# Rows of key differences for the row maxima: later loads, one load for shared keys, and a unit of eleven phases

## The chip, the cores and the metric

One NeuronCore of one Trainium2 chip runs the whole program as a single launch. The metric is the device time of one execution in microseconds. Three runs of the kernel before took 5777.38, 5781.78 and 5785.39 us; their median is 5781.78 us.

## The reference, cut to what matters

Four layers are computed one after another, A, B, A, B. Every layer normalizes its input, projects it, attends with 32 heads of 18 elements over 2048 positions, projects the result and adds it to its input. A layer of kind A has its own keys and values for each head; a layer of kind B has one key head and one value head for all 32 query heads.

```
S, D, H = 2048, 576, 32;  Dh = 18
def _A_ref(x, wqkv, wo):
    q, k, v = (x @ wqkv) split into 3 x 32 heads
    scores = einsum("bhqd,bhkd->bhqk", q, k) * Dh ** -0.5
    p = softmax(scores);  o = einsum("bhqk,bhkd->bhqd", p, v)
    return o @ wo
def _B_ref(x, wq, wk, wv, wo):      # k, v: one head
    scores = einsum("bhqd,bkd->bhqk", q, k) * Dh ** -0.5
    ...
x = x + _A_ref(layernorm(x)); x = x + _B_ref(layernorm(x))
x = x + _A_ref(layernorm(x)); x = x + _B_ref(layernorm(x))
```

All arrays are float32. Queries and keys are held as a high and a low part, so that three products of 18 rows each (54 rows) give a score in nearly full precision in one matmul.

## The kernel before, in words

**Units.** Heads are taken in pairs `p` (16 of them), and the queries in quarters `u` of 512, so that a layer has 64 units `(p, u)`. The two heads of a pair lie in partitions 0 to 63 and 64 to 127 (`a` = 0 or 1), so a matmul for one head and a matmul for the other can run side by side. A unit needs three kinds of TensorE work:

- 32 *max* matmuls (`max_mm`, L557): 128 queries against 512 keys into a PSUM tile `psm` with three buffers. VectorE reduces each to its row maxima (L580). Four of the 32 are *difference* matmuls (L570): the keys are replaced by the difference of the first two key blocks, ScalarE applies a relu (L573), and the other of the two blocks is then added and reduced in one VectorE operation (L578), so that one of two reductions is taken off VectorE. Which of the 32 they are is in `UNIT_X`.
- 32 *exp* matmuls (`exp_mm`, L787 to L797): 128 keys against 512 queries into a PSUM tile `pse` with four buffers, with the row maximum subtracted through two further rows of the query tile. ScalarE writes the exponentials (L797) to `pt`.
- 8 blocks of 512 columns of the *values* product (`pv_block`, L818): four matmuls at a time, in four column groups of the array, accumulate in `oacc`, which ScalarE copies out once a unit (L825).

**Order of the work.** The order is written out by hand in `UNIT`: a list of phases, each a string of max (`m`) and exp (`e`) matmuls with the head that they belong to, followed by a number of columns of the values product. One pass through the list is one unit: 32 `m`, 32 `e`, 4096 columns. The list before has ten phases. Max matmuls run 56 ahead of exp matmuls (`LEAD` = 14 steps of four).

**Small work by due time.** The rest is put into `todo` with a due step (`at`, L868), and `run_todo` issues at the start of a phase what is due; a step is four exp matmuls. For a unit that ends at step `b`: `max_store` at `b + NM_AT` transposes the negated maxima on VectorE (L778) and sends them to DRAM (L780); `max_rows` at `b + ROW_AT` loads them as rows of the query tile (L784); `l_part`, `l_inv`, `l_out`, `l_rows`, `o_mul`, `o_out` make and apply the reciprocal sums with GpSimd and small DMAs. The negated maxima are split into two parts on GpSimd (L158 and L773 into `hl`) before the transpose. All DMAs are issued by the one SyncE queue (SP), in program order.

**Key differences.** For each pair, `diff_in` (L599) loads parts of the keys, `diff_split` (L614) subtracts and splits them on GpSimd, `diff_out` (L624) writes them to DRAM in `kd_d`, and `diff_rows` (L631) loads them from there as 54 rows per head. The rows of pair 0 lie in the ends of two slots of `big`; those of pair `p` > 0 lie in one of two places in `xx`, by `p % 2` (`kd`, L592). In a layer of kind A the four steps of pair `p + 1` are due at steps 32p-10, 32p-7, 32p-5 and 32p-2 (L881); the max matmuls of pair `p - 1`, which read the same place, end at step 32p. In a layer of kind B they run twice, for pairs 0 and 1, though the key head is the same.

Of the kernel before, what the change touches and what calls it, by code (L numbers as in the profile page):

```python
# [17 lines left out]
DH = D // H  # L18
P = 128
NCH = S // P  # L20
NPAIR = H // 2
# [23 lines left out]

STEPS = 8
LEAD = 14
NM_AT = 3
ROW_AT = 5
SUM_AT = 3  # L50
L_AT = 5
# [10 lines left out]

UNIT = [("m0 m1 e0 e1 m1", 256), ("e1 m0 m0 e1 e0 m1", 480), ("m0 e1 m1 e0 e0 m1 e0", 448),
# [3 lines left out]
UNIT = [([(o[0], int(o[1])) for o in rows.split()], cols) for rows, cols in UNIT]  # L69

UNIT_X = (1, 9, 18, 24)


@with_exitstack
def tile_kernel(ctx: ExitStack, tc: tile.TileContext, A_x, A_wqkv, A_wo, B_x, B_wq, B_wk, B_wv, B_wo, out):
    nc = tc.nc
# [313 lines left out]
    for layer in range(4):  # L393
        is_a = layer % 2 == 0
# [79 lines left out]
        def q_slot(p):  # L474
            return (3, 5, 1)[p % 3] if is_a else (3, 4, 0)[p % 3]
# [43 lines left out]
        def ops(p):  # L519
            return big[:, q_slot(p)], big[:, k_slot(p)]  # L520
# [11 lines left out]
        for a in range(2):  # L532
            cycle = [g for rows, _ in UNIT for kind, g in rows if kind == "m"]
            n = -4 * LEAD % 32
            own = [(i, i % 32 in UNIT_X) for i in range(n, n + 32) if cycle[i % 32] == a]
            order = [None] * 16
# [8 lines left out]
        def max_place(a, i):  # L545

            p, u = divmod(i // 16, 4)
            if i < len(m_first):
                return (0, *m_first[i])
            n = i % 16  # L550
            return (p, u, *m_order[a][n]) if i >= 32 else (p, u, n // 2 % 4, n // 8 % 2 * 2 + n % 2)


        ns = STEPS * 4 * NPAIR
        m_heads = ([0, 1] * (2 * LEAD) + [g for rows, _ in UNIT for kind, g in rows if kind == "m"] * (4 * NPAIR))[:4 * ns]

        def max_mm(bank=mtile):  # L557

            i = m_done[0]
            a = m_heads[i]  # L560
            p, u, qc, kb = max_place(a, m_next[a])
            q, k = ops(p)
            if (p, u) not in mxs:
                mxs[p, u] = pool.tile([P, 32], F32, name="mx") if (p, u) < (0, 2) else mx2[u % 2]
            mx, ps = mxs[p, u], bank("psm")
            b, r = 64 * a, 16 * a + 4 * qc + kb
            c0 = u * 512 + qc * P
            if (p, u) >= (0, 2) and (a, qc, kb) in m_diff:
                k = kd(p)[b:b + 3 * DH]
                nc.tensor.matmul(ps.rearrange("p (h t) -> p h t", h=2) if p == 0 else ps, q[b:b + 3 * DH, c0:c0 + P], k,  # L570
                                 start=True, stop=True)
                t = relus[p, u, a, qc] = relu[:, :512]
                nc.scalar.activation(t, ps, AF.Relu)  # L573
            else:
                nc.tensor.matmul(ps, q[b:b + KM, c0:c0 + P], k[b:b + KM, kb * 512:(kb + 1) * 512], start=True, stop=True)  # L575
                if kb == 0 and (p, u, a, qc) in relus:
                    t = relus.pop((p, u, a, qc))
                    nc.vector.tensor_tensor_reduce(t, ps, t, 1.0, LOWEST, OP.add, OP.max, mx[:, r:r + 1])  # L578
                else:
                    nc.vector.reduce_max(mx[:, r:r + 1], ps, axis=AX.X)  # L580
            m_next[a] += 1
            m_done[0] += 1
            while m_full and i >= m_full[0][1] + 2:
                max_final(*m_full.pop()[0])
            m_count[p, u] = m_count.get((p, u), 0) + 1
            if m_count[p, u] == 32:
                assert m_next[0] == m_next[1]
                m_full.append(((p, u), i))

        relus, diffs = {}, {}  # L590

        def kd(p):  # L592
            if p == 0:
                return big[:, 1::4, 7 * 256:]
            i = p % 2 if is_a else 1
            return xx_flat[:, 512 * i:512 * i + 512]


# [30 lines left out]
                nc.sync.dma_start(kd_d[:n, i].rearrange("c (h t) -> c h t", h=2), parts_[:2 * n, c:c + 256])  # L629

        def diff_rows(p):  # L631
            for a in range(2):
                c = a * DH if is_a else 0
                src = kd_d[c:c + DH].rearrange("c i t -> (c i) t")
                if p == 0:
                    src = src.rearrange("r (h t) -> r h t", h=2)
                nc.sync.dma_start(kd(p).bitcast(F32)[64 * a:64 * a + 3 * DH], src)
# [230 lines left out]
        def at(b, f, *args):  # L868
            todo.setdefault(b, []).append((f, args))

        for p in range(NPAIR):
            for u in range(4):
                b = STEPS * (4 * p + u) + STEPS - 1
                if is_a or p or u:
                    at(b + NM_AT, max_store, p, u)
                    at(b + ROW_AT, max_rows, p, u)
                for d, f in ((SUM_AT, o_sum), (L_AT, l_part), (INV_AT, l_inv), (R_AT, l_out), (RB_AT, l_rows),
                             (MUL_AT, o_mul), (O_AT, o_out)):
                    at(b + LEAD + d, f, p, u)
            if p + 1 < NPAIR and (is_a or p == 0):  # L880
                b = max(LEAD, 32 * p - 10)  # L881
                for d, f in ((0, diff_in), (3, diff_split), (5, diff_out), (8, diff_rows)):
                    at(b + d, f, p + 1)
            if is_a and p in (0, 1):
                at(LEAD + 20 + 32 * p, load_rows, q_slot(p + 1), 2 * (p + 1) * DH, DH, 1536, S)
            if p + 1 < NPAIR:
                for i in range(4 if is_a else 2):
                    at(LEAD + 32 * (p - 1) + 1 + 8 * i if p else LEAD + 1 + 4 * i, load_part, p + 1, i)
        for c in range(5):
# [3 lines left out]
            if layer < 3:  # L893
                b = LEAD + 32 * (NPAIR - 1) + 2 * c
# [6 lines left out]
        def run_todo(st):  # L901
            for n in sorted(n for n in todo if n <= st):
                for f, args in todo.pop(n):
                    f(*args)

        b = LEAD + ns
# [10 lines left out]
        e_next = [0, 0]  # L917
# [6 lines left out]
        phase = 0  # L924
        while m_done[0] < 4 * ns:
            rows, cols = UNIT[phase % len(UNIT)]
            run_todo(LEAD + sum(e_next) // 4)
            for kind, a in rows:
                if kind == "e":
                    exp_next(a)  # L930
                elif m_done[0] < 4 * ns:
                    max_mm()
            if phase >= 2:
                pv_cols(cols)
            phase += 1
# [1 line left out]
            max_final(*m_full.pop()[0])  # L937

        while sum(e_next) < 4 * ns:
            run_todo(LEAD + sum(e_next) // 4)  # L940
            for _ in range(min(4, 4 * ns - sum(e_next))):
                exp_next(int(e_next[0] > e_next[1]))
            pv_cols(512)
# [39 lines left out]
```

## Time and profile before

| what | value |
|---|---|
| median of 3 runs | 5781.78 us (5777.38 to 5785.39) |
| the profiled execution | 5788.86 us, of which 5787.0 us are the span of its instructions |
| granted TensorE clock, mean | 0.988 |
| VectorE busy | 4942.6 us (85%) |
| ScalarE busy | 4942.4 us (85%) |
| GpSimd busy | 1839.9 us (32%) |
| DMA queue with the data | 18.2% of 16 engines' span |

How to read the lines that follow: a group of instructions is named by its line in the kernel, its engine and `out<-in`, the tiles that it writes and reads; PE is TensorE's matmuls, PEld its weight loads, DVE VectorE, ACT ScalarE, POOL GpSimd, SPq the queue that issues DMAs. A busy TensorE is not a TensorE at its peak, because a matmul counts from its start to its modelled end and neighbours overlap; the time from one start to the next tells more than a duration. A layer's attention takes most of its time: the first layer's values products run from 220.1 us, and the fourth layer's end at 5731.0 us.

### The profile page before, as it was taken

What the parts mean: (1) busy time and instruction counts of PE and PEld (TensorE: products, weight loads), DVE (VectorE), ACT (ScalarE), POOL (GpSimd) and SP (SyncE); (2) the same over time, 40 slices, a digit from 0 to 9 for tenths busy, and PEclk for the clock granted to TensorE, in tenths of its full rate; (3) what the DMA queues carried; (4) which work ended last, traced back from release to release, by engine and by line L of the source; (5) the groups of instructions that cost most, each with busy time, mean ns of one, the idle gap of its engine ahead of it and who ended that gap; (6) DMA issues with size and microseconds to landing.
All of it is one profiled execution on the core that took longest, in us unless ns stands there. A gap on an engine that the chain in (4) does not pass through costs nothing.

```text
span 5787.0 us, 140436 instructions
## 1 busy us (share of the span) xinstructions
PE 5701.3 (99%) x53790; PEld 2953.2 (51%) x53790; DVE 4942.6 (85%) x9489; ACT 4942.4 (85%) x9872; POOL 1839.9 (32%) x2406
## 2 busy tenths in 40 slices
PE   9999999999999999999999999999999999999999
PEld 8644444444744444444685444444447444444446
DVE  4788988899589999999638888998986899999995
ACT  2599999999479999999626999999993799999996
POOL 3243333333233323323312433333332332332332
PEclk9999999999999999999999999999999999999999
DMA  6321111111321010011253211111113210000002
GB/s 206 114 57 42 39 41 44 42 42 25 110 85 25 22 23 20 23 24 24 59 177 97 51 44 43 39 41 44 42 22 124 72 27 23 20 23 23 20 17 78
DMA packets 276059, 302.44 MB, mean 52 GB/s; under 512 B 135408, under 2 KB 193856, under 8 KB 266096
## 3 DMA queue, kind: packets, MB, share of 16 engines
q1 hardware_dynamic: 275384, 293.45, 18.2%
q8 instruction: 423, 6.93, 0.5%
q14 instruction: 252, 2.06, 0.1%
HBM read 169.23 MB, written 120.08 MB: 50 GB/s over the span
## 4 chain that ended last, share of the span: by engine, by line
PE 93%; DMA 2%; POOL 1%; DVE 1%; issue 1%; SPq 1%; ACT 0%; POOLq 0%; DVEq 0%; ACTq 0%
PE oacc L818 35%; PE pse L793 22%; PE psm L575 20%; PE psn L241 6%; PE psq L415 5%; PE psm L570 4%; DMA xx<-kd_d 1%; DVE mx L580 1%; PE ps L233 0%; DMA m_d<-tr 0%; DMA big<-m_d 0%; POOL big L187 0%; DMA raw<-in_B_wk_dram 0%; SPq L780 0%; POOL ev L427 0%
## 5 line engine op out<-in xcount | busy, mean ns | idle before, releaser
L797 ACT ACTIVATE pt<-pse 128x512 f32<-128x512 f32 x8192 | 4263.7, 635 | 112.8 <-PE psm L575 65.7
L580 DVE TENSOR_REDUCE mx<-psm 128x1 f32<-128x512 f32 x6208 | 3957.4, 685 | 400.5 <-PE psm L575 179.1
L575 PE MATMUL psm<-big 62*128 62x512 f32 x7200 | 2680.6, 457 | 5.5 <-DMA big<-qk_d 3.4
L793 PE MATMUL pse<-big 64*128 64x512 f32 x8192 | 2409.3, 431 | 11.9 <-DMA big<-m_d 10.0
L575 PEld LDWEIGHTS psm<-big 62*128 62x128 f32 x7200 | 1188.2, 186 | 1081.3 <-DVE mx L580 871.4
L818 PE MATMUL oacc<-pt,vbuf 128*19 128x448 f32 (+1 forms) x24560 | 1730.2, 384 | 3.5 <-DVE oc L158 3.5
L793 PEld LDWEIGHTS pse<-big 64*128 64x128 f32 x8192 | 1225.0, 187 | 362.3 <-ACT pt L797 159.8
L158 POOL TENSOR_SCALAR os<-oc 32x512 f32<-32x512 f32 x512 | 313.0, 611 | 2861.2 <-ACT oc L825 2727.1
L818 PEld LDWEIGHTS oacc<-pt,vbuf 128*19 128x19 f32 x24560 | 477.0, 98 | 672.4 <-issue 578.5
L578 DVE CUSTOM_DVE_ANT_0 relu<-psm,relu 128x512 f32<-128x512 f32 x992 | 674.6, 680 | 0.0
L573 ACT ACTIVATE relu<-psm 128x512 f32<-128x512 f32 x992 | 613.3, 618 | 62.2 <-PE psm L570 60.7
L818 PE MATMUL oacc<-pt,vy 128*19 128x352 f32 (+3 forms) x8176 | 588.0, 395 | 0.0
L570 PE MATMUL psm<-xx,big 54*128 54x512 f32 x960 | 454.6, 474 | 47.6 <-DMA xx<-kd_d 47.6
L844 POOL TENSOR_TENSOR rl<-lt,mone 128x8 f32<-128x8 f32 x256 | 422.3, 1650 | 232.8 <-DMA lt<-os 223.6
L570 PEld LDWEIGHTS psm<-xx,big 54*128 54x128 f32 x960 | 177.2, 185 | 398.6 <-DVE mx L580 372.2
L423 ACT ACTIVATE ev<-psq 128x512 fp32r<-128x512 f32 (+1 forms) x112 | 66.9, 598 | 331.7 <-PE psq L415 230.3
L857 POOL TENSOR_TENSOR os<-os,rb 96x512 f32<-96x512 f32 x256 | 329.0, 1285 | 31.3 <-DMA rb<-r_d 30.3
L835 POOL TENSOR_TENSOR os<-os,oc 96x512 f32<-96x512 f32 x256 | 327.7, 1280 | 21.3
L241 PE MATMUL psn<-wsm,xx 128*128 128x288 f32 x2240 | 308.0, 296 | 0.0
L241 PEld LDWEIGHTS psn<-wsm,xx 128*128 128x128 f32 x2240 | 298.7, 188 | 12.9 <-issue 11.3
L818 PEld LDWEIGHTS oacc<-pt,vy 128*19 128x19 f32 x8176 | 182.1, 100 | 194.2 <-issue 171.2
L429 DVE TENSOR_TENSOR ev<-psq,ev 128x512 fp32r<-128x512 f32 (+1 forms) x84 | 57.9, 690 | 213.4 <-ACT ev L423 198.6
(93 smaller groups left out, 2214.3 us busy)
## 6 DMA issues: line engine op xcount, KB each, us to landing
big<-qk_d SPq DMA_DIRECT2D x172, 432.0 KB
qk_d<-ev SPq DMA_DIRECT2D x96, 512.0 KB
qk_d<-ev SPq DMA_DIRECT2D x120, 256.0 KB
rb<-r_d SPq DMA_DIRECT2D x512, 36.0 KB
o_d<-os SPq DMA_DIRECT2D x512, 36.0 KB
m_d<-tr SPq DMA_DIRECT2D x1024, 2.0 KB
o<-o_d SPq DMA_DIRECT2D x64, 256.0 KB
xx<-qk_d SPq DMA_DIRECT2D x120, 72.0 KB
```

Source lines behind the costliest of these rows:

```text
L241: nc.tensor.matmul(ps, lhs[:, xc, :], wsm[:, wc, h * 288:(h + 1) * 288], start=i == 0, stop=i == len(TERMS) - 1)
L570: nc.tensor.matmul(ps.rearrange("p (h t) -> p h t", h=2) if p == 0 else ps, q[b:b + 3 * DH, c0:c0 + P], k, start=True, stop=True)
L573: nc.scalar.activation(t, ps, AF.Relu)
L575: nc.tensor.matmul(ps, q[b:b + KM, c0:c0 + P], k[b:b + KM, kb * 512:(kb + 1) * 512], start=True, stop=True)
L578: nc.vector.tensor_tensor_reduce(t, ps, t, 1.0, LOWEST, OP.add, OP.max, mx[:, r:r + 1])
L580: nc.vector.reduce_max(mx[:, r:r + 1], ps, axis=AX.X)
L793: nc.tensor.matmul(e, k[r:r + KE, kc * P:(kc + 1) * P], q[r:r + KE, u * 512:(u + 1) * 512], start=True, stop=True)
L797: nc.scalar.activation(pt, e, AF.Exp, scale=SCALE)
L818: nc.tensor.matmul(oacc[j:j + DH + 1, cs], v_of(kc)[:, 2 * p + a if is_a else 0, :], pts[p, u, i][:, cs], start=kc < 2 and c0 == 0, stop=k ...
L835: nc.gpsimd.tensor_tensor(t[:96], t[:96], oc[:96], op=OP.add)
L844: nc.gpsimd.tensor_tensor(rl, lts.pop((p, u)), mone, op=OP.pow)
L857: nc.gpsimd.tensor_tensor(t[:96], t[:96], rb[:96], op=OP.mult)
```

## The change

The list of phases is a new one with eleven phases, and the four difference matmuls have other places in it. `NM_AT` becomes 2.5, and the step that `run_todo` compares with is no longer rounded down, so a half step can be told. The key differences of pair `p + 1` are due two steps later, and the load of their rows four steps later (for `p` > 0). In a layer of kind B only pair 0's differences are made, and all pairs use them from the slots of `big`. `kd_pair` is bookkeeping while the program is built and leaves no instruction.

```diff
-NM_AT = 3
+NM_AT = 2.5
-UNIT = [("m0 m1 e0 e1 m1", 256), ("e1 m0 m0 e1 e0 m1", 480), ("m0 e1 m1 e0 e0 m1 e0", 448),
-        ("m0 m1 e1 e0 m0 e1", 192), ("e1 m0 m1 m0 e1", 480), ("e0 m1 e0 e0 m1 m0 e1", 416),
-        ("m0 m1 e1 m0 e1 e0 e1 m1 m0", 480), ("m1 e0 m1 e0 e1 m0", 384), ("m1 e0 e1 m0 m1 e0", 512),
-        ("e1 m0 e0 e1 m0 m1 e0", 448)]
+UNIT = [("m0 e1 e0 m1 e0 m1", 512), ("m0 e1 m1 e0 e1 m0", 416), ("e0 m1 m0 e1 e0 e1 m0", 416),
+        ("m0 m1 e1 e0 m1", 192), ("e1 m0 m1 e0 e1 m0", 544), ("m1 e0 e0 m1 m0 e1", 352), ("e0 m1 e1 m0 m0 e1", 416),
+        ("e0 m1 e0 e1 m1 m0 e1", 384), ("m0 m1", 32), ("e1 m0 e0 e1 e0 m1 m0", 448), ("e1 m0 m1 e0 e0 m1", 384)]
-UNIT_X = (1, 9, 18, 24)
+UNIT_X = (9, 17, 24, 30)
...
-                nc.tensor.matmul(ps.rearrange("p (h t) -> p h t", h=2) if p == 0 else ps, q[b:b + 3 * DH, c0:c0 + P], k,
+                nc.tensor.matmul(ps.rearrange("p (h t) -> p h t", h=2) if p == 0 or not is_a else ps,
+                                 q[b:b + 3 * DH, c0:c0 + P], k,
...
         def kd(p):
-            if p == 0:
+            if p == 0 or not is_a:
                 return big[:, 1::4, 7 * 256:]
-            i = p % 2 if is_a else 1
+            i = p % 2
...
-            if p + 1 < NPAIR and (is_a or p == 0):
-                b = max(LEAD, 32 * p - 10)
-                for d, f in ((0, diff_in), (3, diff_split), (5, diff_out), (8, diff_rows)):
-                    at(b + d, f, p + 1)
+            if p + 1 < NPAIR and is_a:
+                for d, f in ((0, diff_in), (3, diff_split), (5, diff_out), (10 if p else 8, diff_rows)):
+                    at(max(LEAD, 32 * p - 8) + d, f, p + 1)
...
-            run_todo(LEAD + sum(e_next) // 4)
+            run_todo(LEAD + sum(e_next) / 4)
```

More of the change, by code (lines that the diff above doesn't have):

```diff
@@ L568, in max_mm @@
             if (p, u) >= (0, 2) and (a, qc, kb) in m_diff:
+                assert kd_pair[p % 2 if is_a and p else 2] == (p if is_a else 0)
                 k = kd(p)[b:b + 3 * DH]
-                nc.tensor.matmul(ps.rearrange("p (h t) -> p h t", h=2) if p == 0 else ps, q[b:b + 3 * DH, c0:c0 + P], k,
+                nc.tensor.matmul(ps.rearrange("p (h t) -> p h t", h=2) if p == 0 or not is_a else ps,
+                                 q[b:b + 3 * DH, c0:c0 + P], k,
                                  start=True, stop=True)
@@ L588, in max_mm @@
                 m_full.append(((p, u), i))
-        relus, diffs = {}, {}
+        relus, diffs, kd_pair = {}, {}, {}
         def kd(p):
-            if p == 0:
+            if p == 0 or not is_a:
                 return big[:, 1::4, 7 * 256:]
-            i = p % 2 if is_a else 1
+            i = p % 2
             return xx_flat[:, 512 * i:512 * i + 512]
@@ L631, in diff_rows @@
         def diff_rows(p):
+            kd_pair[p % 2 if p else 2] = p
             for a in range(2):
@@ L939, in tile_kernel @@
         while sum(e_next) < 4 * ns:
-            run_todo(LEAD + sum(e_next) // 4)
+            run_todo(LEAD + sum(e_next) / 4)
             for _ in range(min(4, 4 * ns - sum(e_next))):
```

## The prediction

> **What bounds the kernel now.** I read the busy shares first, then who waits for whom on TensorE, then windows of the two kinds of layer, then the timeline of one unit.
>
> ```profile
> PE 5701.3 (99%) x53790; PEld 2953.2 (51%) x53790; DVE 4942.6 (85%) x9489; ACT 4942.4 (85%) x9872; POOL 1839.9 (32%) x2406
> PE psm L570 <- DMA xx<-kd_d: 47.6, 26, 2.9
> PE pse L793 <- DMA big<-m_d: 10.0, 7, 3.0
> ```
>
> TensorE is never idle for long, so every microsecond has to be found either in its few waits or in the way its matmuls follow one another. Its largest wait is for the rows of key differences: 26 times, 47.6 us. The difference matmul is written after the load that overwrites its place, so it reads, and waits for, the rows of a later pair. Whether it costs more than those 47.6 us is told by the exp matmuls (32 to a unit) that a long window holds. The first and third windows lie in layers of kind A, the others in kind B:
>
> ```profile
> 340.00:1290.00 950.00, 458.58 (x1529) 234.93 (x1529) 0.97 0.16 42
> 1660.00:2820.00 1160.00, 573.40 (x1974) 292.44 (x1972) 1.00 0.10 24
> 3220.00:4240.00 1020.00, 492.76 (x1647) 251.93 (x1645) 0.98 0.16 41
> 4545.00:5700.00 1155.00, 570.75 (x1966) 291.42 (x1963) 1.00 0.09 22
> PE psm L570 <- DMA xx<-kd_d: 21.1, 12, 2.9
> PE psm L570 <- DMA xx<-kd_d: 21.2, 12, 2.4
> ```
>
> The last two rows are the waits within the first and third window, 12 in each. Columns of the others: window, length, PE busy and count, weight loads, granted clock, DMA. A unit takes 950 x 32/1529 = 19.88 us and 1020 x 32/1647 = 19.82 us in A, but (1160 + 1155) x 32/(1974 + 1966) = 18.80 us in B. At B's pace the two A windows would be 950 - 898.4 = 51.6 and 1020 - 967.7 = 52.3 us shorter: 103.9 us for 24 waits, 4.3 us each, though one wait is 1.8 us. The rest is in the clock:
>
> ```profile
> 410.01 0.50 PE L575 MATMUL psm<-big 62*128 62x512 f32 x1
> 412.05 0.47 PE L570 MATMUL psm<-xx,big 54*128 54x512 f32 x1 [1.54 <-DMA xx<-kd_d]
> 412.00:413.00 1.00, 0.95 (x4) 0.60 (x4) 0.00 (x0) 0.45 (x1) 0.00 (x0) 0.91 0.52 164
> 413.00:416.00 3.00, 3.00 (x27) 1.50 (x30) 1.71 (x3) 2.18 (x6) 0.00 (x0) 0.50 0.33 98
> 416.00:417.00 1.00, 1.00 (x10) 0.14 (x4) 0.87 (x3) 0.55 (x2) 0.00 (x0) 0.88 0.00 0
> ```
>
> After a gap of 1.54 us the granted clock is 0.50 for three microseconds, and for 0.18 and 0.24 us of its neighbours: 3.42 us, half of them lost. With a start 1.70 us late (a next matmul follows after 0.34 us, see below), this boundary costs 1.70 + 1.71 = 3.41 us.
>
> One unit of a B layer, where nothing of this happens, shows what a phase costs:
>
> ```profile
> 2005.82 0.50 PE L570 MATMUL psm<-xx,big 54*128 54x512 f32 x1
> ...
> 2007.56 1.00 PE L818 MATMUL oacc<-pt,vbuf 128*19 128x480 f32 x8
> 2008.49 0.50 PE L575 MATMUL psm<-big 62*128 62x512 f32 x1
> ...
> 2009.41 0.85 PE L818 MATMUL oacc<-pt,vbuf 128*19 128x32 f32 x16
> 2010.18 0.50 PE L575 MATMUL psm<-big 62*128 62x512 f32 x1
> ...
> 2010.52 0.40 PE L575 MATMUL psm<-big 62*128 62x512 f32 x1
> ...
> 2011.11 1.06 PE L818 MATMUL oacc<-pt,vbuf 128*19 128x160 f32 x16
> 2012.10 0.50 PE L793 MATMUL pse<-big 64*128 64x512 f32 x1
> ...
> 2013.25 0.95 PE L818 MATMUL oacc<-pt,vbuf 128*19 128x160 f32 x16
> 2000.58:2019.45 18.87, 18.87 (x197) 8.77 (x194) 17.83 (x35) 18.56 (x38) 5.76 (x8) 1.00 0.14 34
> ```
>
> Starts matter. Matmuls of the two heads share a slot; the second slot begins 0.34 us after the first (2010.18 to 2010.52). A string of three slots takes 0.92 us (2008.49 to 2009.41; 0.93 from 2010.18), one of four 1.15 us (2012.10 to 2013.25). So n slots cost about 0.23 + 0.23n. The values products take 0.93 us for 480 columns, 0.77 for 384, 0.99 for 512: 0.13 us and 0.00167 us a column. The last row is the whole unit: 18.87 us, in which VectorE is busy for 17.83 and ScalarE for 18.56 us.
>
> **The change part by part.** *The later rows.* At four steps later the load comes two steps after the last matmul of the pair that had the place, and the listing of the changed program's instructions has a DMA among the awaited events of 10 difference matmuls instead of 37, none at the regular pair boundaries. Each of the 26 waits is worth between 3.41 us (the boundary above) and 4.3 us (the mean over 24): 89 to 113 us. I take 108, near the mean, and a little less because those windows may hold other short losses. What is late next is nothing that I can find: the rows now land 30 steps before their first use. On SP the pair's loads, `kd_d` writes and rows are the same DMAs, two to four steps later.
>
> [...]
>
> *One load where there is one key head.* This removes 9 DMAs and 5 GpSimd operations in each B layer. They lie at its beginning, in front of row loads that an exp matmul awaits:
>
> ```profile
> 1646.41 2.48 SPq L629 DMA_DIRECT2D kd_d<-xx  x3
> ...
> 1650.56 0.53 SPq L784 DMA_DIRECT2D big<-m_d  x2
> 1651.14 0.50 PE L570 MATMUL psm<-big 54*128 54x512 f32 x1
> 1654.54 0.66 PE L793 MATMUL pse<-big 64*128 64x512 f32 x2 [2.91 <-DMA big<-m_d]
> 1655.00:1658.70 3.70, 3.70 (x29) 1.51 (x31) 2.15 (x4) 2.58 (x5) 0.00 (x0) 0.54 0.36 105
> L570 PE MATMUL psm<-xx,big 54*128 54x512 f32 x960 | 454.6, 474 | 47.6 <-DMA xx<-kd_d 47.6
> L570 PE MATMUL psm<-big 54*128 54x512 f32 x32 | 15.1, 472 | 0.0
> ```
>
> The exp matmul starts 1654.54 - (1651.14 + 0.34) = 3.06 us late, and 3.70 us at clock 0.54 lose 1.70 more: 4.8 us. Without the 2.48 us of writes ahead of it the row load is issued that much earlier, and earlier still for want of the reads in front of the store; that removes most of the gap and with it the slow clock. Two B layers: 0 to 10 us, I take 8. That all pairs now read the strided rows in `big` costs nothing: 472 ns against 474.
>
> *The eleven phases.* Slots by counting the strings, with a matmul going into the current slot unless its head is there already: before six strings of three, three of four, one of five; now seven of three, three of four, one of one. Without waits, before: 6 x 0.92 + 3 x 1.15 + 1.38 + 10 x 0.13 + 4096 x 0.00167 = 18.49 us; the measured 18.87 has 0.38 more, and the nine-matmul string alone shows 1.74 - 1.38 = 0.36 (2005.82 to 2007.56). Now: 7 x 0.92 + 3 x 1.15 + 0.46 + 11 x 0.13 + 6.84 = 18.62 us. The eleventh phase thus costs 0.36 us in fixed parts, a slot less returns 0.23, and the wait of the long string is what can be won. Why it waits:
>
> ```profile
> 2004.43 1.88 DVE L580 TENSOR_REDUCE mx<-psm 128x1 f32<-128x512 f32 x3
> 2006.23 0.20 DVE L778 STREAM_TRANSPOSE tr<-hl 128x32 f32<-128x32 f32 x1
> 2006.39 1.93 DVE L580 TENSOR_REDUCE mx<-psm 128x1 f32<-128x512 f32 x3
> ...
> 2009.03 1.29 DVE L580 TENSOR_REDUCE mx<-psm 128x1 f32<-128x512 f32 x2
> 2006.37 0.50 PE L575 MATMUL psm<-big 62*128 62x512 f32 x1
> 2002.44 0.20 POOL L773 TENSOR_TENSOR hl<-neg,hl 128x8 fp32r<-128x8 f32 x1
> ```
>
> Three reductions take 1.88 us, one every 0.60 us, and the last ends (2006.31) 0.06 us before the max matmul that takes its buffer (2006.37). Five max matmuls in one string want five reductions in the time of 1.38 + 0.93 us, and there are three buffers. The new list has three in ten phases and two in the ninth. I went through it with these spacings (a reduction starts 0.55 us after a first slot, as at 2009.03 after 2008.49, and frees its buffer 0.68 + 0.05 us after its start). Phases 7 and 8 pinch most: phase 7 begins at 0, its three reductions start at 0.55, 1.15 and 1.76 and the last frees its buffer at 2.49; phase 8 begins at 0.92 + 0.13 + 416 x 0.00167 = 1.75 and wants it in its third slot, at 2.32: 0.17 us late. Four other places come out at 0.02 to 0.05 us. I take 0.20, so 18.82 us, 0.05 less than now. Bounds: no wait, 18.62; the old wait in full, 19.00. The list runs (2048 - 56)/32 = 62.25 times a layer, 249 in all: -62 to +32 us, I take -12. The single-slot phase is shown by no row; 0.46 is drawn from the others, and 0.1 more would be 25 us.
>
> *Transposes half a step earlier.* They move from phase 7 to the beginning of phase 6, in front of that phase's reductions, and their store moves ahead of the two loads of `l_part` on SP, which then wait for it; GpSimd's reciprocal comes later by some 2 us and is hidden, as GpSimd is busy for only 5.76 of 18.87 us. `hl` is ready at 2002.64, 2.1 us after the beginning of phase 4 (2000.58); in the new list phases 4 and 5 take 0.92 + 0.13 + 0.32 and 0.92 + 0.13 + 0.91, so phase 6 begins 3.3 us after phase 4 and VectorE does not wait. Cost nothing; the row loads get up to 1.7 us more room.
>
> Sum: 5788.9 for the profiled execution - 108 - 8 - 12 = 5661. The span lies 1.9 us below that execution's time and the median 7.1 us below it; the forecast for the median is 5781.8 - 128 = 5654 us.
>
> **The rivals.** *The boundary wait returns elsewhere.* The pair's loads still crowd SP at each boundary, and the row loads that exp matmuls await (7 waits before) could be next, with the slow clock behind them. For: one gap is enough for the price. Against: the `kd_d` writes no longer stand between store and row load of a unit. Half of 108 back: 5708.
>
> *The clock falls at the boundaries anyway*, because gaps as short as these do not cause it: only the late starts are won, 26 x 1.70 = 44 instead of 108: 5718. Against it stands that it falls within 0.8 us of the gap. [...]
>
> *The new list is dearer*: the single-slot phase costs 0.1 more and every phase waits as the long one did, 19.1 us a unit: +57 instead of -12, so 5723. [...]
>
> *Slower: VectorE held by the transposes.* VectorE works in order; if GpSimd delivers `hl` after VectorE arrives at phase 6, its reductions stand still, three buffers fill and TensorE stops. It has 1.04 us to spare in a unit. It decides once `hl` comes 1.2 us later than now; the gain of 116 us is gone when a unit loses 0.47 us beyond the spare. A hold of 2 us gives 249 x 0.96 - 116 = +123: 5905.
>
> *It does not do what it says*: the boundary waits stay, 5762. The instruction listing speaks against it.
>
> **How the numbers follow.** Forecast 0.70 (5654; its own range goes from 5600, with the list at -62 and the waits at 113, to 5717, with the list at +32 and the waits at 89); returned wait 0.08; the clock falling anyway 0.04; dearer list 0.08; held VectorE 0.08; waits stay 0.02. The range of 5598 to 5712 holds nearly all of the forecast and most of the returned wait; it leaves out VectorE held, the waits that stay, and about half of the clock falling anyway and of the dearer list. Below 0.2% (12 us) a measurement cannot tell a change. All cases but the held VectorE are faster by more, and of its 0.08 a short hold may come out even: faster 0.92, same 0.01, slower 0.07.
>
> **What would show it.** Right: no row of L570 waiting for `xx<-kd_d`, granted clock 1.00 in the A windows, A units as long as B units, the first exp matmuls of a B layer without the 2.91 us gap, and 18.6 to 19.0 us for a unit. Wrong: waits for `big<-m_d` or `big<-qk_d` with clock 0.50 behind them, TensorE waiting for the single-slot phase's neighbours, or idle time of VectorE before L778 ended by GpSimd.

## The result, and the profile after

The changed kernel takes 5687.06 us (median of 4 runs, 5681.73 to 5689.18) against 5781.66 us (4 runs, 5777.38 to 5785.39): the ratio is 0.9835, with a 95% interval of 0.9818 to 0.9852. The forecast was 5654 us with a range of 5598 to 5712: the direction and the range held, and the gain was 95 us where 128 were expected.

The profiled execution took 5685.8 us, 103 us less than the one before. It lies 1.3 us below the median of its runs, where the one before lay 7.2 us above its own: the medians therefore differ by 8 us less than the profiles.

First the busy shares of the kernel after:

```profile
PE 5650.3 (99%) x57758; PEld 3010.8 (53%) x57758; DVE 4917.2 (87%) x9489; ACT 4932.6 (87%) x9872; POOL 1836.8 (32%) x2396
```

Then the largest waits of its TensorE for DMAs, in us, times and the longest:

```profile
PE psm L576 <- DMA big<-qk_d: 4.0, 2, 2.1
...
PE pse L795 <- DMA big<-m_d: 2.2, 3, 1.4
```

No difference matmul (L570) waits for its rows any more. The windows over the exp matmuls, now L795, are read as those of before: 890 x 32/1508 = 18.89 us for a unit of the first layer, then 18.83, 18.86 and 18.83 us, and the clock is 1.00 in all four.

```profile
400.00:1290.00 890.00, 445.02 (x1508) 220.43 (x1507) 1.00 0.17 44
1660.00:2770.00 1110.00, 556.10 (x1886) 275.16 (x1886) 1.00 0.10 24
3220.00:4110.00 890.00, 445.45 (x1510) 220.70 (x1508) 1.00 0.17 44
4545.00:5600.00 1055.00, 528.24 (x1793) 261.58 (x1793) 1.00 0.09 21
```

So layers of kind A run at B's pace, as forecast. B's own pace has not improved, and there most of the 33 us that were not won must be looked for. From the start of a layer's first values product to the start of its last, the four layers took 1263.4, 1210.0, 1263.0 and 1212.3 us before and 1213.7, 1207.2, 1213.4 and 1207.0 us after: 107.4 us less in all. Outside these stretches 4.4 us came back, which makes the 103 us.

The next table is worked out from the start times in the traces: the median over a layer's units of the time from the first matmul of a string to the values product behind it, by phase, and their sum; then the sum of the eleven (ten) values products, and the median unit. The kernels called by a label are those of the experiments.

| kernel | strings by phase, us | sum | values | unit |
|---|---|---|---|---|
| before | .91 .90 1.13 .91 .98 1.13 1.74 .91 .93 1.14 | 10.68 | 8.17 | 18.86 |
| after | .90 1.02 1.13 .98 .91 1.00 .91 1.20 .43 1.13 .97 | 10.58 | 8.30 | 18.89 |
| e8_no_sum | .90 1.01 1.13 .98 .91 .99 .92 1.20 .43 1.13 .92 | 10.52 | 8.30 | 18.83 |
| e9_half | .91 .90 1.13 .89 1.02 .90 1.01 1.14 .43 1.13 .90 | 10.36 | 8.30 | 18.68 |
| e10_old_half | .91 .90 1.13 .90 .90 1.13 1.70 .90 .95 1.14 | 10.56 | 8.17 | 18.72 |
| e11_old_columns | .92 .93 1.13 .90 .93 1.13 1.74 .90 .95 1.14 | 10.67 | 8.47 | 19.13 |
| e12_half_relu | .90 .90 1.13 .90 .90 1.13 1.48 .90 .89 1.13 | 10.26 | 8.17 | 18.45 |

The eleven phases made a unit 0.03 us longer instead of 0.05 us shorter. The string of nine matmuls (1.74) is gone, but five strings, those of phases 2, 4, 6, 8 and 11, are 0.06 to 0.11 us longer than the same number of slots is elsewhere (0.91 and 1.14): 0.39 us together.

Phase 2 shows what such a place looks like. These rows are the timeline of TensorE's matmuls, then of its weight loads, then of VectorE, in a layer of kind B of the kernel after; each has start, duration, engine, line, operation and tiles, and the idle time before it with what ended it.

```profile
1907.60 0.49 PE L576 MATMUL psm<-big 62*128 62x512 f32 x1
...
1907.94 0.40 PE L576 MATMUL psm<-big 62*128 62x512 f32 x1
...
1908.19 0.49 PE L576 MATMUL psm<-big 62*128 62x512 f32 x1
1908.62 0.89 PE L820 MATMUL oacc<-pt,vbuf 128*19 128x416 f32 x8
```

```profile
1907.71 0.19 PEld L576 LDWEIGHTS psm<-big 62*128 62x128 f32 x1
...
1908.19 0.18 PEld L576 LDWEIGHTS psm<-big 62*128 62x128 f32 x1
```

```profile
1907.45 0.68 DVE L579 CUSTOM_DVE_ANT_0 relu<-psm,relu 128x512 f32<-128x512 f32 x1
```

The second max matmul has its weights loaded 0.23 us ahead (1907.71 for 1907.94). The third takes the buffer that VectorE frees at 1907.45 + 0.68 = 1908.13. Its matmul is hardly late: 0.59 us after the first, where 0.57 is usual. But its weight load does not run ahead: it starts at 1908.19 with the matmul, 0.06 us behind the buffer, so the values product follows 0.43 us behind instead of 0.33. In this trace 1045 weight loads of L576 have a wait that VectorE's L581 ends, 231.6 us in all.

The medians over all units say the same. In the kernel after, the weights of the last max matmul of a string are loaded 0.00 to 0.03 us ahead of it in phases 2, 4, 6, 8 and 11, and what comes behind the string follows that matmul by 0.40 to 0.43 us. In the other strings of three and four slots the load is 0.09 to 0.18 us ahead, and the product follows by 0.32 to 0.34 us. In e9_half, where VectorE frees the buffers sooner, the load of phases 2, 4, 6 and 11 is 0.23 us ahead, and the product follows by 0.32 to 0.33 us.

Something that cost less before stands near the end of each A layer, where GpSimd prepares the next layer's weights. These are the rows of several engines around a gap in the first layer, and the windows behind it (the engines' busy times, then the clock):

```profile
1301.34 0.41 POOL L157 TENSOR_SCALAR big<-raw 128x256 fp32r<-128x256 f32 x1 [3.06 <-DMA raw<-in_B_wk_dram]
...
1305.33 1.58 ACT L799 ACTIVATE pt<-pse 128x512 f32<-128x512 f32 x3 [2.39 <-POOL os L837]
...
1305.98 0.50 PE L795 MATMUL pse<-big 64*128 64x512 f32 x1 [1.18 <-ACT pt L799]
1306.04 0.21 DVE L780 STREAM_TRANSPOSE tr<-hl 128x32 f32<-128x32 f32 x1 [2.52 <-POOL hl L775]
```

```profile
1307.00:1308.00 1.00, 1.00 (x4) 0.67 (x5) 1.00 (x2) 1.00 (x3) 0.00 (x0) 0.68 0.34 88
1308.00:1310.00 2.00, 2.00 (x19) 0.27 (x16) 1.40 (x3) 1.36 (x3) 0.00 (x0) 0.50 0.09 13
1310.00:1312.00 2.00, 2.00 (x25) 1.25 (x23) 1.01 (x2) 1.05 (x3) 0.36 (x1) 0.81 0.07 7
```

GpSimd waited 3.06 us for a weight DMA, and two engines then waited for GpSimd. ScalarE stood still for 2.39 us until the sum of L837 had read `oc`, because `pt` and `oc` share their buffers (`ptile`); VectorE's transposes waited 2.52 us for the negated maxima. TensorE ran dry: its gap of 1.18 us ended when ScalarE freed a buffer of `pse`, and 0.64 + 2.00 + 0.76 = 3.4 us of half clock lie behind it. That unit takes 22.8 us, and its counterpart in the third layer 24.4; before they took 19.5 and 22.4, and in the second of these ScalarE had waited 2.3 us for the same sum. This costs 5 us over the two layers.

### The profile page after: what moved, and what is told of

It is laid out like the page before. It is cut to its first block, busy times and chain, and to the rows that moved or that the text cites. A ratio compares the mean times of both kernels' runs of the same rounds, so it can differ in the third digit from the quotient of the medians.

```text
span 5684.0 us, 148130 instructions
## 1 busy us (share of the span) xinstructions
PE 5650.3 (99%) x57758; PEld 3010.8 (53%) x57758; DVE 4917.2 (87%) x9489; ACT 4932.6 (87%) x9872; POOL 1836.8 (32%) x2396
## 4 chain that ended last, share of the span: by engine, by line
PE 95%; POOL 1%; DMA 1%; issue 1%; DVE 1%; SPq 0%; ACT 0%; POOLq 0%; DVEq 0%; ACTq 0%
PE oacc L820 37%; PE pse L795 23%; PE psm L576 18%; PE psn L240 6%; PE psm L570 5%; PE psq L414 5%; DVE mx L581 1%; PE ps L232 0%; POOL big L186 0%; DMA raw<-in_B_wk_dram 0%; DMA m_d<-tr 0%; DMA big<-qk_d 0%; DMA big<-m_d 0%; DMA qk_d<-ev 0%; POOL ev L426 0%
## 5 line engine op out<-in xcount | busy, mean ns | idle before, releaser
L581 DVE TENSOR_REDUCE mx<-psm 128x1 f32<-128x512 f32 x6208 | 3931.1, 685 | 313.0 <-PE psm L576 132.7
L576 PE MATMUL psm<-big 62*128 62x512 f32 x7200 | 2665.8, 452 | 7.1 <-DMA big<-qk_d 4.0
L795 PE MATMUL pse<-big 64*128 64x512 f32 x8192 | 2411.4, 429 | 5.6 <-ACT pt L799 3.3
L820 PE MATMUL oacc<-pt,vbuf 128*19 128x96 f32 (+3 forms) x27536 | 1754.9, 361 | 3.5 <-DVE oc L157 3.5
L795 PEld LDWEIGHTS pse<-big 64*128 64x128 f32 x8192 | 1191.8, 185 | 784.5 <-ACT pt L799 602.3
L576 PEld LDWEIGHTS psm<-big 62*128 62x128 f32 x7200 | 1164.1, 184 | 381.4 <-DVE mx L581 231.6
L820 PEld LDWEIGHTS oacc<-pt,vbuf 128*19 128x19 f32 x27536 | 530.2, 98 | 782.2 <-issue 652.0
L820 PE MATMUL oacc<-pt,vy 128*19 128x256 f32 (+3 forms) x9168 | 591.4, 360 | 0.0
L820 PEld LDWEIGHTS oacc<-pt,vy 128*19 128x19 f32 x9168 | 206.0, 98 | 267.9 <-issue 220.0
L837 POOL TENSOR_TENSOR os<-os,oc 96x512 f32<-96x512 f32 x256 | 327.0, 1277 | 21.4
L570 PE MATMUL psm<-big 54*128 54x512 f32 x512 | 240.7, 470 | 0.0
L570 PE MATMUL psm<-xx,big 54*128 54x512 f32 x480 | 225.0, 469 | 0.0
```

Of the source, the lines that this page charges most:

```text
L795: nc.tensor.matmul(e, k[r:r + KE, kc * P:(kc + 1) * P], q[r:r + KE, u * 512:(u + 1) * 512], start=True, stop=True)
L820: nc.tensor.matmul(oacc[j:j + DH + 1, cs], v_of(kc)[:, 2 * p + a if is_a else 0, :], pts[p, u, i][:, cs], start=kc < 2 and c0 == 0, stop=k ...
L837: nc.gpsimd.tensor_tensor(t[:96], t[:96], oc[:96], op=OP.add)
```

## The experiments

All ratios are to the kernel before on the same chip, with the 95% interval; these runs of the kernel before have medians of 5785.7 to 5789.2 us.

**e1_list_only: the kernel before with the new list.** The edit is the part of the diff with `UNIT` and `UNIT_X`, and nothing else.

> The kernel before with the new list of eleven phases and its UNIT_X alone. Theory: the new list alone removes the boundary waits as well, because its last difference matmul of a unit is max matmul 22 of 32 (index 30 of the list), while the rows are loaded at max matmul 24; the old list's stood at 25, behind the load. So 5782 - 108 for the waits + 8 for a unit of 18.89 instead of 18.86 us: about 5682, with no wait of a difference matmul for kd_d. Rival: the later load is what removed them, and the list alone gives 5782 + 8 = 5790.

Measured: 5698.83 us, 0.9848 (0.9834 to 0.9861), 87 us less where the theory had 100. Windows of the first and third layer, exp matmuls:

```profile
400.00:1290.00 890.00, 444.86 (x1507) 220.59 (x1507) 1.00 0.17 44
3220.00:4110.00 890.00, 444.62 (x1507) 220.60 (x1507) 1.00 0.17 44
```

The waits are gone: 890 x 32/1507 = 18.90 us a unit, clock 1.00. The new list alone also removes the waits that the forecast put down to the later load; that its difference matmuls lie elsewhere in the unit fits, but was not tried by itself. The first units of the B layers are still long (23.1 and 23.5 us).

**e2_rows_only: the kernel before with the later loads alone.**

```diff
-                b = max(LEAD, 32 * p - 10)
-                for d, f in ((0, diff_in), (3, diff_split), (5, diff_out), (8, diff_rows)):
+                b = max(LEAD, 32 * p - 8)
+                for d, f in ((0, diff_in), (3, diff_split), (5, diff_out), (10 if p else 8, diff_rows)):
```

> The kernel before with the key differences two steps and their rows four steps later, nothing else. Theory: each of the 26 waits costs its late start and the half clock behind it, about 4.2 us, so 5782 - 108 = 5674, with a granted clock of 1.00 in the A windows. Rival: the clock falls at the boundaries for another reason, then only the late starts are won: 5782 - 44 = 5738.

Measured: 5683.94 us, 0.9826 (0.9812 to 0.9841), 102 us less. The same windows:

```profile
400.00:1290.00 890.00, 440.01 (x1511) 224.79 (x1509) 1.00 0.17 44
3220.00:4110.00 890.00, 440.11 (x1512) 224.84 (x1510) 1.00 0.17 43
```

So the later loads suffice too, and are worth about the 108 us of the forecast, slow clock included. The two edits are not additive: the 87 us of e1_list_only and these 102 us are mostly the same waits.

**e3_old_list: the changed kernel with the old list.** `UNIT` and `UNIT_X` as before, everything else as after. **e4_nm3** and **e6_old_list_nm3** are the kernel after and e3_old_list with `NM_AT` = 3, that is without the transposes' half step.

> The changed kernel with the old list of ten phases and its UNIT_X: later rows, one load in B, transposes half a step earlier. Theory: the later load alone removes the waits, and the old list is 0.03 us a unit quicker (18.86 against 18.89, 249 units): 5687 - 8 = 5679. Transposes half a step earlier now stand in phase 6, before the long string of phase 7, whose reductions they may push back by their 0.2 us: up to 249 x 0.1 = 25 more, 5704. Rival: the new list is worth the 12 us that were predicted, then 5699 without any push.

> The changed kernel with NM_AT = 3. Theory: once in each A layer VectorE is held by a transpose that waits for GpSimd, with the slow clock behind it (units of 22.78 and 24.43 us instead of 18.89: 3.9 and 5.5 us); half a step later it would not wait: 5687 - 9 = 5678, and nothing else moves. Rival: the earlier transposes pay elsewhere (row loads that exp matmuls await), then 5687 or more.

> The changed kernel with the old list and NM_AT = 3, that is the kernel before with the later rows and the one load in B. Theory: 5782 - 108 - 11 = 5663, quicker than both kernels; a unit of 18.86 us, no unit above 20 us at a pair boundary. Rival: without the new list the loads still collide at the boundaries, and half of the 108 stays: 5717.

Measured: e3_old_list 5675.31 us, 0.9808 (0.9795 to 0.9822); e4_nm3 5683.07, 0.9825 (0.9812 to 0.9839); e6_old_list_nm3 5677.52, 0.9813 (0.9800 to 0.9827). With the old list the kernel is 12 us faster than with the new one (5675.31 against 5687.06; the two intervals overlap by a hair, and the units, 18.85 against 18.89, say the same). The half step is worth nothing that can be told in either direction with either list. In e4_nm3 VectorE waits only 0.9 us at the place near the end of the first layer, but ScalarE still waits 2.1 us for GpSimd's sum, and the unit still takes 22.2 us; its counterpart in the third layer takes 20.2. Of all kernels that compute the full row maxima, e3_old_list has the lowest time; e6_old_list_nm3, 2 us behind it and 14 us above its own theory, can't be told from it.

**e5_one_load: the kernel before with a single load in B layers.**

```diff
-            if p == 0:
+            if p == 0 or not is_a:
                 return big[:, 1::4, 7 * 256:]
...
-            if p + 1 < NPAIR and (is_a or p == 0):
+            if p + 1 < NPAIR and is_a:
```

> The kernel before with one load of key differences in a B layer, nothing else. Theory: the first units of the two B layers (23.64 and 25.23 us) fall to 18.86: -11, 5771. Rival: the row load that the exp matmul awaits is late for another reason: the early transposes removed that wait, and this alone gives -2 or less: 5780.

Measured: 5780.12 us, 0.9988 (0.9978 to 0.9997), 6 us less over 10 runs. The first units of the B layers fall from 23.6 and 25.2 to 19.3 and 18.9 us, which is 11 us in this execution. The wait of exp matmuls for `big<-m_d` at that place is gone, while in e1_list_only and e2_rows_only it is still there with 2.3 to 2.7 us: this edit removes it, and neither the new list nor the later rows do. The earlier transposes were not tried alone.

**e7_rows_sooner: the gap without the slow clock?** The kernel before, with the rows loaded two steps sooner instead of later.

```diff
-                for d, f in ((0, diff_in), (3, diff_split), (5, diff_out), (8, diff_rows)):
+                for d, f in ((0, diff_in), (3, diff_split), (5, diff_out), (6 if p else 8, diff_rows)):
```

> The kernel before with the rows loaded two steps sooner (6 instead of 8 behind diff_in), so that they stand in front of one small DMA on SP and are issued about 0.75 us earlier, and the difference matmul still waits for them. Theory: the gaps shrink from 1.8 to about 1.1 us, and the clock falls only behind gaps of more than about 1.2 us (gaps of 0.6 and 1.0 in the trace of before had none behind them, those of 1.3 to 2.9 all had): 26 x 0.75 = 20 for the starts and the greater part of the 26 slow stretches of 1.7 to 3.4 us, about 45: near 5715. Rival: the clock falls at these places whatever the gap: 5782 - 20 = 5762.

Measured: 5738.45 us, 0.9917 (0.9902 to 0.9931), between the two. At the boundaries of the first layer TensorE now has gaps of 0.70 to 1.88 us, eight ended by the rows and five, of 0.72 to 0.87 us, by VectorE. Here is a row of the timeline with one of them, then windows of 4 us around and behind the end of three of them (PE busy, clock, DMA); these gaps are 1.61, 1.18 and 1.88 us:

```profile
333.39 0.47 PE L570 MATMUL psm<-xx,big 54*128 54x512 f32 x1 [1.61 <-DMA xx<-kd_d]
```

```profile
333.00:337.00 4.00, 3.61 (x36) 1.00 0.57 152
...
642.00:646.00 4.00, 3.70 (x30) 0.64 0.42 114
...
1105.00:1109.00 4.00, 3.20 (x30) 0.79 0.52 132
```

Only 2 of the 13 gaps of that layer have a slow clock behind them, and it isn't the length that decides: a gap of 1.74 us at 565.25 has none, one of 1.18 us has it. The units with a gap and the full clock take 20.0 to 21.1 us, 1.2 to 2.2 us more than the others, which is the late start alone; the two with the slow clock take 21.97 and 22.78 us, 3.1 and 3.9 us more. Both parts of the price that the forecast put on a wait are thus real, and they come apart. But "one gap is enough" is not a rule.

The records of the granted clock in the traces, from which the views take their clock column, show what the length leaves out. In the kernel before and in the kernel after the changes of the clock lie on a grid of 3.413 us, to within 0.01 us, over the whole trace. In this kernel the two slow stretches begin at 643.08 and 1107.30, 136 x 3.413 us apart. On the grid through these times the gaps of 1.18 and 1.88 us each lie within one interval, while a grid point at 564.57 cuts the gap of 1.74 us into 1.06 and 0.68 us. The kernel before has such a case too: its gap of 2.30 us that ends at 3373.14 is cut into 1.34 and 0.96 us and has no slow clock behind it; the other 25 gaps there all have. The length within one interval does not decide either: 1.32 us, ended at 487.39, brought no slow clock.

**e8_no_sum: is it the sum with relu that is late?** The kernel after, with a plain reduction in the place of the sum:

```diff
-                    nc.vector.tensor_tensor_reduce(t, ps, t, 1.0, LOWEST, OP.add, OP.max, mx[:, r:r + 1])
+                    nc.vector.reduce_max(mx[:, r:r + 1], ps, axis=AX.X)
```

> The changed kernel with a plain row maximum in place of the sum with relu (the difference block is left out of the maximum), which takes about 0.13 us from each of four VectorE operations of a unit. Theory: the strings of phases 2, 4, 6, 8 and 11 are 0.06 to 0.11 us longer than strings of their size elsewhere because their last max buffer comes free too late for its weight load to run ahead; three of them (2, 6, 11) follow a sum with relu, and lose their 0.11 + 0.10 + 0.06: 249 x 0.27 = 67, so 5620, or half of it if other buffers take their place. Rival: the strings are longer for a reason in TensorE itself (the order of heads, the change of shape): 5687.

Measured: 5669.52 us, 0.9801 (0.9785 to 0.9818). Only phase 11 gives way (0.97 to 0.92 us); phases 2 and 6 keep their 1.01 and 0.99. My first theory of the late places fell: it isn't the kind of VectorE instruction, for a plain reduction in its place comes just as late.

**e9_half: VectorE out of the way, with the new list.** **e10_old_half: the same with the old list.** Both lines of the row maxima read half of the tile.

```diff
-                    nc.vector.tensor_tensor_reduce(t, ps, t, 1.0, LOWEST, OP.add, OP.max, mx[:, r:r + 1])
+                    nc.vector.tensor_tensor_reduce(t[:, :256], ps[:, :256], t[:, :256], 1.0, LOWEST, OP.add, OP.max, mx[:, r:r + 1])
-                    nc.vector.reduce_max(mx[:, r:r + 1], ps, axis=AX.X)
+                    nc.vector.reduce_max(mx[:, r:r + 1], ps[:, :256], axis=AX.X)
```

> The changed kernel, with VectorE reducing only 256 of the 512 columns of every max tile (half of the keys are left out of the row maxima), so that buffers of psm come free some 0.3 us sooner and VectorE is never late. Theory (all that the new list loses beside its slots are third slots whose buffer VectorE frees just in time): the strings of phases 2, 4, 6, 8 and 11, now 1.02, 0.98, 1.00, 1.20 and 0.97 us, return to about 0.91 (phase 8: 1.14), 0.40 us a unit, so 18.89 - 0.40 = 18.49 us and 5687 - 249 x 0.40 = 5587 us. Rival (they are late for ScalarE's buffers or for the change between kinds of matmul): strings and time stay, 5687 us. The forecast's bound without any wait, 18.62 us a unit, would give 5620 us.

> The changed kernel with the old list of ten phases (5675 us) and the same halved reductions. Theory: the nine-matmul string falls from 1.74 to 1.38 us and phase 5 from 0.98 to 0.91, so 0.43 us a unit: 18.85 - 0.43 = 18.42 us and 5675 - 107 = 5568 us, which is 0.07 us a unit (some 19 us) below the same kernel with the new list; the eleventh phase then costs more in fixed parts than the slot that it saves, with no VectorE wait in either list. Rival: the two lists come out even or the new one ahead once VectorE is out of the way, 5587 us or more.

Measured: e9_half 5625.09 us, 0.9720 (0.9704 to 0.9736); e10_old_half 5632.23, 0.9731 (0.9717 to 0.9746). In the new list all five late strings return to about 0.90 and to 1.14 us, as the theory has it: 0.44 us. But the unit falls by only 0.21, for two other strings, those of phases 5 and 7, grow by 0.10 each. Weight loads, first their waits in the kernel after, then in e9_half, then two rows of e9_half's timeline in phases 5 and 7:

```profile
PEld pse L795 <- ACT pt L799: 602.3, 1192, 2.6
...
PEld psm L576 <- DVE mx L581: 231.6, 1045, 0.7
```

```profile
PEld pse L795 <- ACT pt L799: 707.4, 1753, 1.9
...
PEld psm L576 <- DVE mx L581: 46.5, 266, 0.8
```

```profile
1912.95 0.18 PEld L795 LDWEIGHTS pse<-big 64*128 64x128 f32 x1 [0.20 <-ACT pt L799]
...
1916.62 0.18 PEld L576 LDWEIGHTS psm<-big 62*128 62x128 f32 x1 [0.27 <-ACT relu L574]
```

Once VectorE is quick, ScalarE ends the waits: an exp matmul waits for a buffer of `pse`, and a max matmul for the buffer that holds a difference block. The old list was the surprise: its string of nine barely moved (1.74 to 1.70 us), and its unit fell by 0.13 instead of 0.43. With VectorE out of the way the new list is 0.04 us a unit ahead, though the intervals of the two times overlap.

**e12_half_relu: why the string of nine waits.** e10_old_half, and the relu of the difference block halved too:

```diff
-                nc.scalar.activation(t, ps, AF.Relu)
+                nc.scalar.activation(t[:, :256], ps[:, :256], AF.Relu)
```

> The old list with halved reductions (5632 us), and ScalarE's relu of the difference block halved too, to 256 columns. Theory (the fifth slot of the nine-matmul string waits for the relu of the difference matmul that opens the string, whose buffer it takes, and not for VectorE): the relu, 0.63 us, ends 0.2 to 0.3 us sooner, so that string falls from 1.70 to 1.40 to 1.50 us and the unit from 18.72 to 18.42 to 18.52 us: 249 x 0.2 to 0.3 = 50 to 75 us less, 5557 to 5582 us. Rival (the five slots are slow by themselves, or the exp matmuls' buffers hold the string): it stays at 1.70 us, 5632 us.

Measured: 5565.65 us, 0.9612 (0.9596 to 0.9628), 67 us below e10_old_half, and the string falls to 1.48 us. Its last two max matmuls take the buffers of the difference matmul that opens it and of its neighbour; the first of these is freed by ScalarE. Weight loads in that string of e10_old_half, and ScalarE's relu there:

```profile
2008.54 0.18 PEld L571 LDWEIGHTS psm<-big 54*128 54x128 f32 x1 [0.69 <-DVE mx L582]
...
2009.81 0.18 PEld L577 LDWEIGHTS psm<-big 62*128 62x128 f32 x2 [0.31 <-ACT relu L575]
```

```profile
2009.13 0.63 ACT L575 ACTIVATE relu<-psm 128x512 f32<-128x512 f32 x1
```

2009.13 + 0.63 = 2009.76, and the loads start 0.05 us later. The matmuls of the string in e12_half_relu, its first and its last, and the halved relu:

```profile
1986.11 0.50 PE L571 MATMUL psm<-big 54*128 54x512 f32 x1
...
1987.16 0.50 PE L577 MATMUL psm<-big 62*128 62x512 f32 x2
```

```profile
1986.69 0.41 ACT L575 ACTIVATE relu<-psm 128x256 f32<-128x256 f32 x1
```

With the half relu, 0.41 us, the last two start 1.05 us after the first, where it was 2009.81 - 2008.54 = 1.27. They still start 0.06 us behind the end of the relu (1986.69 + 0.41 = 1987.10), so the string waits for it even now. In the median over 248 units that distance is 0.05 us in the kernel before and in e10_old_half and 0.06 us in e12_half_relu. The half relu was tried only together with the halved reductions; with the full ones the row of the kernel before, shown further below, has the same releaser.

**e11_old_columns: more room ahead of a late third slot.** e3_old_list with the values columns moved between phases, the strings unchanged:

```diff
-UNIT = [("m0 m1 e0 e1 m1", 256), ("e1 m0 m0 e1 e0 m1", 480), ("m0 e1 m1 e0 e0 m1 e0", 448),
-        ("m0 m1 e1 e0 m0 e1", 192), ("e1 m0 m1 m0 e1", 480), ("e0 m1 e0 e0 m1 m0 e1", 416),
+UNIT = [("m0 m1 e0 e1 m1", 192), ("e1 m0 m0 e1 e0 m1", 480), ("m0 e1 m1 e0 e0 m1 e0", 480),
+        ("m0 m1 e1 e0 m0 e1", 224), ("e1 m0 m1 m0 e1", 512), ("e0 m1 e0 e0 m1 m0 e1", 416),
-        ("m0 m1 e1 m0 e1 e0 e1 m1 m0", 480), ("m1 e0 m1 e0 e1 m0", 384), ("m1 e0 e1 m0 m1 e0", 512),
+        ("m0 m1 e1 m0 e1 e0 e1 m1 m0", 480), ("m1 e0 m1 e0 e1 m0", 384), ("m1 e0 e1 m0 m1 e0", 480),
```

> The changed kernel with the old list of ten phases (5675 us), whose matmul strings stay while the columns of the values products between them move: 192, 480, 480, 224, 512, 416, 480, 384, 480, 448 in place of 256, 480, 448, 192, 480, 416, 480, 384, 512, 448. Theory (a third slot is late only by what VectorE lacks, and more columns ahead of it give VectorE that time): phases 4 to 6, which had a string of 0.98 us in phase 5, get 0.05 us each and phase 5 returns to 0.91, while phase 1, which waits for nothing, gives up 0.11 us of room: 0.03 to 0.07 us a unit less, 5659 to 5668 us. Rival (columns only move the wait on to the next string): the time stays, 5675 us.

Measured: 5739.37 us, 0.9916 (0.9901 to 0.9931): 64 us more than e3_old_list, a miss. The string in question did what the theory says (0.98 to 0.93 us). But the values products grew by 0.30 us a unit, in phase 6 (0.82 to 0.91) and above all in phase 7 (0.93 to 1.15), whose columns are the same in number. They now begin 96 columns further on and so reach into the next block of 512, whose exponentials belong to the string just ahead. ScalarE, matmuls and weight loads of phase 7:

```profile
2010.04 2.08 ACT L800 ACTIVATE pt<-pse 128x512 f32<-128x512 f32 x4
```

```profile
2010.76 1.22 PE L821 MATMUL oacc<-pt,vbuf 128*19 128x416 f32 x16
```

```profile
2010.76 0.14 PEld L821 LDWEIGHTS oacc<-pt,vbuf 128*19 128x19 f32 x8 [0.25 <-issue]
...
2011.49 0.32 PEld L821 LDWEIGHTS oacc<-pt,vbuf 128*19 128x19 f32 x6 [0.24 <-issue]
```

The four exponentials start 0.48 us apart; the third ends at 2010.04 + 0.96 + 0.63 = 2011.63. Of the last six weight loads two start at 2011.49 and the other four only at 2011.68, 0.05 us behind it. The two products cost 249 x 0.31 = 77 us, more than the 64 measured; the shorter string in phase 5 gives some of it back. A product that is cut in two needs the exponentials of its second block, so the columns are not free to move.

## Why the prediction was right, and which term was mis-sized

- **The waits.** Right in size and in kind: 108 us forecast; in the trace the long units at the pair boundaries of the A layers, which exceeded 18.86 us by 107.0 us in all, are gone, and e2_rows_only won 102 us with this edit alone. The clock records of the kernel before give the same sum by its parts: behind the 26 gaps lie 18 stretches of half clock of 3.41 us and 7 of 6.83 us, which lose half of their time, 54.6 us; with 47.6 us of gaps, and an estimated 26 x 0.16 us by which a start is later than its gap is long (1.70 against 1.54 us at the boundary of the forecast), that is 106 us. Not seen was that the new list removes the same waits by itself (e1_list_only). The step that priced a wait at one gap and one stretch of half clock was right as a mean. Single waits differ: some have two stretches' length behind them, one has none, and e7_rows_sooner shows the two prices apart. The rival of a clock that falls anyway is refuted by the windows of e2_rows_only, 1.00 throughout. What the forecast held against that rival, that the clock falls within 0.8 us of the gap, is true of its one example only: it falls between 0.6 us before and 1.8 us after the end of a gap. The rival's premise, that gaps as short as these do not cause the slow clock, is borne out by no run: in the kernel before it begins within 1.8 us of the end of 25 of the 26 gaps, which last 1.26 to 2.92 us, and in e7_rows_sooner it follows one of 1.18 us, though 11 of the 13 gaps in the first layer there have none.
- **One load in B.** Forecast 8 us; 11 us in the profiled stages, 6 in the medians (e5_one_load). Right, and the place was the one named.
- **The eleven phases.** This is the term that was off: -12 us forecast, some +8 us by the traces (249 x 0.03), +12 us by e3_old_list. Its counting held: the single-slot string takes 0.43 us (0.46 estimated) and its 32 columns 0.18. Two steps failed. The first is "why it waits", where the last of three reductions was taken as what delays the string of nine. That reduction ends just before the third slot, which is on time (2006.37 - 2005.82 = 0.55 us); the late one is the fifth. The trace of before had the answer, in the weight loads of the same string and in their waits:

```profile
2007.08 0.23 PEld L575 LDWEIGHTS psm<-big 62*128 62x128 f32 x2 [0.31 <-ACT relu L573]
```

```profile
PEld psm L575 <- ACT relu L573: 76.3, 248, 0.3
```

  Once a unit (248 times) it is ScalarE's relu that ends this wait, and e10_old_half and e12_half_relu show it: VectorE alone out of the way leaves 1.70 us, the half relu 1.48. This did no harm to the gain, since the new list's strings are short enough for the relu (12 such waits of weight loads are left, with 2.0 us), so that 0.36 us was won as forecast; with the wrong engine named, that is luck. The second step, "0.17 us late" in phase 8 and "four other places ... 0.02 to 0.05", sized the late slots at 0.20 us where they measure 0.39: phase 8 only 0.06, but the other four 0.06 to 0.11. The reckoning asked when the matmul can start and not when its weight load can, and a buffer freed just in time costs the exposed load, 0.43 instead of 0.33 us behind the last max matmul in phase 2. e9_half shows that VectorE is the cause of all five. Both bounds of the term, -62 and +32 us, held.
- **Transposes half a step earlier.** Cost nothing, as forecast: e4_nm3 and e6_old_list_nm3 lie within the noise of their partners. The rival of a VectorE held by the transposes does happen, but in one unit of each A layer, where GpSimd is late behind a weight DMA. There the same GpSimd holds ScalarE as well, which is what ends TensorE's gap, and in e4_nm3 still makes the unit of the first layer long. These two units take 5 us more than before.
- **The other rivals.** No wait returned at the boundaries. A dearer list came in part, 0.03 us a unit, but not by a surcharge for the single-slot phase: no run shows the 0.1 us that this rival puts on it, and its string takes 0.43 us where 0.46 was reckoned.
- **The sum.** In the profiles: -107 for the waits, -11 for B, +8 for the list, +5 for those two units and +4 between the layers make -101 of the 103 us measured; 2 us are not placed. That the profile of before lay 7.2 us above its median, and that of after 1.3 us below, takes 8 more off the medians' difference.
- **Left open.** Why 4 us came back between the layers was not tried. Nor was it tried whether the new list removes the boundary waits by the places of its difference matmuls.

## What to carry to other kernels

When TensorE is full and VectorE and ScalarE nearly so, ask for each slot of a hand-written order which engine frees its buffer, and when the weight load, not the matmul, can start. Read the weight loads' rows as well as the matmuls': the releaser stands there. Before crediting an edit with a wait's removal, look whether another edit of the same change removes it too, and try the parts alone: here the version without the new list is the best one.

## What the runs showed of the hardware

In the kernel after, a buffer that came free 0.04 us before its matmul's usual start (1908.13 for 1907.60 + 0.57) cost 0.1 us (0.43 instead of 0.33), though the matmul itself was late by 0.02: the weight load, which for the last max matmul of an undisturbed string runs 0.09 to 0.18 us ahead in that kernel, started with the matmul, at 1908.19. And the slow clock did not follow the length of a gap. The changes of the granted clock lie on a grid of 3.413 us in the traces of the kernels before and after, and the slow stretches behind their gaps last 3.41 or 6.83 us. Gaps of 1.61 and 1.74 us in e7_rows_sooner and one of 2.30 us in the kernel before, each cut by the grid, passed at full clock, while 1.18 us within one interval brought the slow clock.
